# Block inverses on GpSimd instead of VectorE, the cubic on VectorE, and first blocks turned by VectorE transposes

## The chip, the core and the metric

One core of a Trainium2 chip runs the whole program. Five engines work side by side, each with its own in-order queue: TensorE (PE, with its weight loads PEld), VectorE (DVE), ScalarE (ACT), GpSimd (POOL) and SyncE (SP), which issues most DMAs. The metric is device time in microseconds of one launch, the median of several runs.

## The reference

Three layers follow each other, in float32. The first is delta-rule attention over 768 positions, for 4 batches of 8 heads with dimension 48; per position t

```python
v_old = np.einsum('bhde,bhd->bhe', state, kt)
state = state + bt[:, :, :, None] * np.einsum('bhd,bhe->bhde', kt, vt - v_old)
```

with normalised keys and output `q . state` taken ahead of the update. Its output, 3072 tokens of 384 values, goes through an expert layer of width 2048 with a rational activation, g = (a0 + a1 h + a2 h^2 + a3 h^3) / (1 + |b0| |h| + |b1| h^2 + 1e-6), and then through a second one with g = max(h, 0)^2.

## The kernel before

**Attention.** The sequence is cut into 12 chunks of 64 positions. A chunk of one batch is a step n (48 steps, all 8 heads together), and 8 steps are a group g (6 groups, `attention(g)`). In a chunk the recurrence becomes a solve with a triangular 64 x 64 matrix; per group its 32 x 32 diagonal blocks are inverted, one block in each partition of Tt, by elimination. For groups 2 to 5 that is 31 steps of two operations on DVE (L471 the product into tmp, L472 the subtraction from Tt), with a x b columns, a = s + 1, b = 31 - s; each needs the one before. For groups 0 and 1 the inversion stops at 16 x 16 blocks (15 steps, L462 and L464), and matmuls merge them (`ma`, `mb`, `mc`, L528 to L552, in halves hf). The inverses lie one per partition and are needed as matmul operands, so Tt goes to DRAM (td) and comes back with rows on partitions (L490, L505 into TT); its transpose, which ACT makes in Gb (L491), goes by nd to DN or TN (L508 to L516). Matmuls L578 and L591 with copies L584 and L596 give the 32 x 32 block below the diagonal. Then the steps run: `first`, `middle` (copies L699, masks on POOL L703), `rest` (L724, L738, L743), which write the tokens into xin. The Gram matrices of later groups (L425 and `gram`) go by Gs and DRAM to Gb.

**Layers 1 and 2.** Tokens are taken 512 at a time (i, 6 blocks), hidden units 128 at a time (j, 16). A unit (i, j) of layer 1 is 9 matmuls into a PSUM bank of pool h (3 banks; L866), the rational activation, and 3 second matmuls of full float32 (L904) into three accumulators. In `rational`, ACT makes |h| (L883), a copy hs of h in SBUF (L884) and b0 + b1|h| (L885); POOL multiplies that by |h| (L886), and makes a2 + a3 h (L887) and its product with h (L889) from hs; DVE adds a1 and multiplies (L890), ACT makes 1/Q by Ln and Exp (L891, L892), DVE does the last three operations (L893 to L895). Layer 2 starts when layer 1 is done; its weights are split by ACT and POOL (L824 to L832) ahead of it.

**Order.** All work is entered as tasks by `add(engine, cost, function, r, w, due, ...)`. `Plan.run` plays the list with the costs given, per engine, by due times; it repeats that 8 times, each time with due times worked back from the last play, and emits the instructions in the order of the best one. So each engine's order is fixed when the program is built. A task with `lock=1` on DVE and one on POOL never overlap in the plan. `inv_due(g)` asks for group g's inverse some 90 to 10 us ahead of unit block g - 1, `step_due` spreads the steps over block g - 1. In planned PE gaps of the prologue `PL.fill` puts matmuls on a constant tile (L284, filler).

Of the kernel before, what the change touches and what calls it, by code (L numbers as in the profile page):

```python
# [19 lines left out]
C = 64  # L20
# [15 lines left out]
ROUNDS = 8  # L36
# [11 lines left out]
class Plan:  # L48
# [38 lines left out]
    def run(self):  # L87
# [22 lines left out]
        lo, hi, one, dur = self.fill  # L110
# [116 lines left out]
def kernel(ctx, tc, kT, kS, qT, kn, vn, beta, par_in, w1, w2, outT):  # L227
# [56 lines left out]
    PL.fill = (T0 - 55, T0 + 20, lambda: nc.tensor.matmul(banks[2][:, 0:N // 2], ones[:, 0:128], ones, start=True, stop=True), 0.11)  # L284
# [11 lines left out]
    tiny = at.tile([128, 1], F32, name="tiny")  # L296
    be = at.tile([128, 32], F32, name="be")
# [6 lines left out]
    tiles(at, "kTc", 3, [128, NP, C])  # L304
# [33 lines left out]
    add("POOL", 1.0, eye, w=["ident"], due=15)  # L338
    add("POOL", 1.0, lambda: P_.memset(Nb, 0.0), w=[("N", o) for o in range(0, 128, 32)], due=3)
# [38 lines left out]
    for n in range(8):  # L378
# [22 lines left out]
        add("ACT", 0.6, o2, r=[key], w=[("TN", 32), ("TN", 96)], due=n + 8, free=[key])  # L401
# [12 lines left out]
    def gstore(n, due):  # L414
        add("ACT", 0.37, lambda: A_.copy(slot["Gs", n], ps(("G", n), [128, NP, C])), r=[("G", n)], w=[("Gs", n)], due=due,
            alloc=(("Gs",), ("Gs", n)), free=[("G", n)])
        dma(128, gs[n // 8][:, n % 8], lambda: slot["Gs", n], r=[("Gs", n)], w=[("gs", n)], due=due, free=[("Gs", n)])

    def attention(g):
# [70 lines left out]
        dma(512, td[g], Tt, r=["Tt"], w=[("td", g)], due=d1, lat=2.0)  # L490
        add("ACT", 2.05, lambda: A_.copy(Gb, Tt.rearrange("p a b -> p b a")), r=["Tt"], w=GB, due=d1)  # L491
# [10 lines left out]
        for i in (1, 0):  # L502
# [17 lines left out]
        for hf in range(2 if g < 2 else 0):  # L520
            ka, kb, kc = ("mA", g, hf), ("mB", g, hf), ("mC", g, hf)

            def ma(hf=hf):
                w = ps(("mA", g, hf), [128, 4, NP, 32])
                for s in range(4):
                    for p in range(NP):
                        for o in range(0, 128, 32):
                            M.matmul(w[o:o + 32, s, p], Nb[o:o + 32, 4 * hf + s, p], TTg[o:o + 32, 4 * hf + s, p, o % 64:o % 64 + 32],  # L528
                                     start=True, stop=True)
# [36 lines left out]
            add("PE", 1.3, mc, r=["E"] + dn_, w=[kc], due=dd, alloc=(pl, kc), free=["merge"])
            add("ACT", 1.2, mco, r=[kc], w=[("TNh", hf, 0), ("TNh", hf, 1)], due=dd, free=[kc])


        for hf in range(2):  # L570
# [29 lines left out]
            add("PE", 1.3, m1, r=g21 + [("TTx", g % 2, 1, 0), ("TTx", g % 2, 1, 1), ("TD", g % 2, hf)], w=[kw], due=dd, alloc=(pl, kw))  # L600
            add("ACT", 1.2, m1o, r=[kw], w=["ws"], due=dd, free=[kw])
            add("PE", 1.3, m2, r=[("TN", 0), ("TN", 64), ("TNh", hf, 0), ("TNh", hf, 1), "ws"], w=[kt_], due=dd, alloc=(pl, kt_))
            add("ACT", 1.2, m2o, r=[kt_], w=[("T", g % 2, hf)], due=dd, free=[kt_],
                after=[i for x in range(2) for i in [PL.last["TTx", g % 2, 0, x]]])

# [68 lines left out]
        def first(k, k2, due):  # L674
# [201 lines left out]
    def rational(i, j, due):  # L876
# [3 lines left out]
        hk, ak, bk, ck, gk, sk = (x + (u,) for x in (("h",), ("a",), ("b",), ("c",), ("g",), ("hs",)))  # L880
        h, a, b, c, g, hs = (lambda k=k: slot[k] for k in (hk, ak, bk, ck, gk, sk))
# [3 lines left out]
        add("ACT", 0.83, lambda: A_.activation(b(), a(), AF.Identity, bias=s(4), scale=s(5)), r=[ak, "par"], w=[bk], due=due + 3.8, alloc=(("b",), bk))  # L885
        add("POOL", 1.32, lambda: P_.tensor_tensor(b(), b(), a(), op=ALU.mult), r=[ak], w=[bk], due=due + 5, lock=1)  # L886
# [164 lines left out]
```

## Time and profile before

| | us |
|---|---|
| median of 3 runs (1182.72 to 1186.74) | 1183.78 |
| the profiled execution | 1189.82 |
| its span | 1188.1 |
| PE busy in it | 1088.5 (92%) |
| DVE busy | 716.0 (60%) |
| ACT busy | 676.3 (57%) |
| POOL busy | 459.2 (39%) |
| mean granted PE clock | 0.945 |

The profiled execution is one of its own, so sums made from its rows stand against 1189.82. A span includes all from the first to the last instruction. Line numbers (L471) are those of the kernel before. In the chain of waits, a piece "DMA" is a transfer that something waited for, "SPq" time in SP's queue, "issue" time in which an engine waited for nothing that the profile shows.

### The profile page before, as it was taken

How to read it: one execution, taken by the hardware profiler on the slowest of the kernel's cores; microseconds unless marked ns; L12 is line 12 of the kernel's file. 1: busy time of each engine (PE TensorE's matmuls, PEld its weight loads, DVE VectorE, ACT ScalarE, POOL GpSimd, SP SyncE). 2: the span in 40 equal slices, each digit the busy share in tenths (PEclk: the TensorE clock that was granted, in tenths of full speed). 3: DMA queues.
4: the chain of work that ended last, by engine and by line, in shares of the span. 5: the costliest groups of instructions: out<-in, count | busy, mean ns of one | idle time of the engine just before them, and what ended most of it. 6: DMA issues, size and time to landing. Idle time of an engine off the chain costs nothing.

```text
span 1188.1 us, 24846 instructions
## 1 busy us (share of the span) xinstructions
PE 1088.5 (92%) x10030; PEld 769.2 (65%) x10030; DVE 716.0 (60%) x1237; ACT 676.3 (57%) x1269; POOL 459.2 (39%) x479
## 2 busy tenths in 40 slices
PE   4687898799897998998899989999999999999998
PEld 4576565456554555655566646567788888888887
DVE  4353777887888689668755546788633343333432
ACT  5365876586667576765576867766523333243432
POOL 3304654476564565565456648735300000000000
PEclk7668998799998899998999999999999999999999
DMA  7756324461226033502130022144100001000000
GB/s 223 175 186 162 85 65 144 142 152 40 84 80 126 15 86 87 109 9 59 54 81 17 20 83 80 33 154 138 67 9 27 27 18 36 1 27 1 27 1 27
DMA packets 135394, 87.83 MB, mean 74 GB/s; under 512 B 102384, under 2 KB 119920, under 8 KB 135280
## 3 DMA queue, kind: packets, MB, share of 16 engines
q1 hardware_dynamic: 134992, 85.20, 26.0%
q8 instruction: 79, 1.29, 0.5%
q10 hardware_dynamic: 288, 1.05, 0.2%
q14 instruction: 35, 0.29, 0.1%
HBM read 64.98 MB, written 19.92 MB: 71 GB/s over the span
## 4 chain that ended last, share of the span: by engine, by line
PE 72%; DVE 8%; issue 5%; DMA 4%; ACT 4%; POOL 3%; SPq 3%; ACTq 0%; POOLq 0%; DVEq 0%
PE bank L866 28%; PE bank L904 18%; PE bank L930 5%; PE bank L928 5%; PE bank L929 5%; PE bank L666 5%; SPq L316 3%; DVE tmp L471 2%; PE bank L724 2%; DVE Tt L472 2%; POOL A L825 1%; POOL C L832 1%; DMA kTg<-in_kS_dram 1%; DVE mem L893 1%; PE bank L578 1%
## 5 line engine op out<-in xcount | busy, mean ns | idle before, releaser
L866 PE MATMUL bank<-xh,A 128*128 128x512 f32 x1152 | 362.8, 396 | 3.6 <-POOL A L825 3.6
L904 PE MATMUL bank<-mem,B 128*128 128x512 f32 x576 | 289.0, 635 | 22.1 <-DVE mem L895 21.1
L866 PE MATMUL bank<-xl,A 128*128 128x512 f32 x576 | 258.7, 449 | 11.0 <-DVE mem L895 6.5
L866 PEld LDWEIGHTS bank<-xh,A 128*128 128x128 f32 x1152 | 219.9, 191 | 67.0 <-issue 15.1
L904 PEld LDWEIGHTS bank<-mem,B 128*128 128x128 f32 x576 | 107.6, 198 | 126.3 <-issue 88.7
L916 DVE SCALAR_TENSOR_TENSOR mem<-bank,mem 128x512 f32<-128x512 f32 x96 | 66.3, 691 | 152.2 <-ACT mem L915 152.1
L887 POOL TENSOR_SCALAR mem<-hs,par 128x512 f32<-128x512 f32 x96 | 79.6, 829 | 176.8 <-ACT hs L884 140.5
L866 PEld LDWEIGHTS bank<-xl,A 128*128 128x128 f32 x576 | 110.1, 191 | 54.3 <-issue 14.8
L915 ACT ACTIVATE mem<-bank 128x512 f32<-128x512 f32 x96 | 57.5, 599 | 152.2 <-PE bank L866 152.1
L886 POOL TENSOR_TENSOR mem<-mem 128x512 f32<-128x512 f32 x96 | 126.4, 1317 | 9.3 <-DVE mem L893 4.2
L889 POOL TENSOR_TENSOR mem<-mem,hs 128x512 f32<-128x512 f32 x96 | 125.4, 1306 | 7.4
L930 PE MATMUL bank<-gh,C 128*128 128x512 f32 x288 | 113.7, 395 | 0.0
L928 PE MATMUL bank<-gl,C 128*128 128x512 f32 x288 | 113.5, 394 | 0.0
L929 PE MATMUL bank<-gh,C 128*128 128x512 f32 x288 | 112.0, 389 | 0.0
L893 DVE SCALAR_TENSOR_TENSOR mem<-mem,par,bank 128x512 f32<-128x512 f32 x96 | 71.5, 745 | 61.0 <-ACT bank L892 60.6
L890 DVE SCALAR_TENSOR_TENSOR mem<-mem,par,bank 128x512 f32<-128x512 f32 x96 | 71.1, 741 | 59.4 <-POOL mem L889 56.0
L919 DVE TENSOR_TENSOR gl<-mem,gh 128x512 fp32r<-128x512 f32 x96 | 69.2, 722 | 60.0 <-ACT gh L918 60.0
L918 ACT CAST gh<-mem 128x512 fp32r<-128x512 f32 x96 | 59.6, 621 | 70.9 <-DVE mem L916 59.8
L883 ACT ACTIVATE mem<-bank 128x512 f32<-128x512 f32 x96 | 57.4, 598 | 73.2 <-PE bank L866 72.1
L891 ACT ACTIVATE mem<-mem,par 128x512 f32<-128x512 f32 x96 | 69.2, 721 | 29.2 <-POOL mem L886 28.5
L885 ACT ACTIVATE mem<-mem,par 128x512 f32<-128x512 f32 x96 | 78.5, 817 | 0.9
L703 POOL TENSOR_SCALAR_AFFINE_SELECT X<-X 64x256 f32<-64x256 f32 x96 | 42.0, 438 | 71.1 <-ACT X L699 64.4
(119 smaller groups left out, 1636.7 us busy)
## 6 DMA issues: line engine op xcount, KB each, us to landing
raw<-in_w_dram SPq DMA_DIRECT2D x18, 768.0 KB, 5.3
B<-in_w_dram SPq DMA_DIRECT2D x10, 768.0 KB, 4.8
kTg<-in_kS_dram SPq DMA_DIRECT2D x40, 128.0 KB, 2.9
gs<-Gs SPq DMA_DIRECT2D x40, 128.0 KB, 2.6
kTc<-in_kT_dram SPq DMA_DIRECT2D x40, 128.0 KB, 2.1
kn<-in_kn_dram SPq DMA_DIRECT2D x12, 384.0 KB, 3.7
X<-in_qT_dram SPq DMA_DIRECT2D x96, 48.0 KB, 2.4
vn<-in_vn_dram SPq DMA_DIRECT2D x12, 384.0 KB, 3.2
```

The lines of the kernel that those rows point to most:

```text
L866: M.matmul(h, a, b, start=(k == 0 and m == 0), stop=(k == NK - 1 and m == 2))
L885: add("ACT", 0.83, lambda: A_.activation(b(), a(), AF.Identity, bias=s(4), scale=s(5)), r=[ak, "par"], w=[bk], due=due + 3.8, alloc=(("b", ...
L886: add("POOL", 1.32, lambda: P_.tensor_tensor(b(), b(), a(), op=ALU.mult), r=[ak], w=[bk], due=due + 5, lock=1)
L887: add("POOL", 0.85, lambda: P_.tensor_scalar(c(), hs(), s(3), s(2), op0=ALU.mult, op1=ALU.add), r=[sk, "par"], w=[ck], due=due + 5, lock=1 ...
L889: add("POOL", 1.32, lambda: P_.tensor_tensor(c(), c(), hs(), op=ALU.mult), r=[sk], w=[ck], due=due + 6.5, lock=1, free=[sk])
L890: add("DVE", 0.775, lambda: V.scalar_tensor_tensor(c(), c(), s(1), h(), op0=ALU.add, op1=ALU.mult), r=[hk, "par"], w=[ck], due=due + 7.3)
L891: add("ACT", 0.72, lambda: A_.activation(a(), b(), AF.Ln, bias=s(6)), r=[bk, "par6"], w=[ak], due=due + 7)
L893: add("DVE", 0.775, lambda: V.scalar_tensor_tensor(c(), c(), s(0), h(), op0=ALU.add, op1=ALU.mult), r=[hk, "par"], w=[ck], due=due + 9)
L904: M.matmul(acc[d], Bw[j][:, 128 * d:128 * d + 128], slot[gk], start=(j == 0), stop=(j == NJ - 1))
L928: M.matmul(acc[d], wh, gl, start=(j == 0), stop=False)
L929: M.matmul(acc[d], wl, gh, start=False, stop=False)
L930: M.matmul(acc[d], wh, gh, start=False, stop=(j == NJ - 1))
```

## The change

- The 62 elimination operations of groups 2 to 5 are issued on GpSimd, as two tasks a step.
- In `rational` the copy hs goes. ACT makes a2 + a3 h from the PSUM bank into c, DVE multiplies c by h from the bank; the rest is as before. Due times of the later operations come up to 1 us earlier.
- Groups 0 and 1: td, nd and their ten DMAs go. Two DVE transposes turn the 16 x 16 inverses: from Tt to Gb (then the moving operand of `ma`) and to DN. For group 0 the block Nb is made by ACT, Dg times a column `half` of zeros and ones, in place of four DMAs.
- For group 0 the copies from PSUM with o >= 64 go to DVE (`move`), as does L398; for the others they stay on ACT. Each partition range is a task of its own.
- The transposed keys kTc get a fourth buffer (hs's space is free). Filler matmuls: other constants; `FILL` is 0, so the added minimum does nothing.

```diff
-ROUNDS = 8
+ROUNDS, FILL = 8, 0
...
                 gap = T[i]["s"] - max(end, lo)
-                if gap > 0.6 and T[i]["s"] < hi:
-                    for _ in range(int(0.7 * (gap - 0.2) / dur)):
-                        one()
+                n = int((gap - 0.2) / dur) if gap > 0.5 and T[i]["s"] < hi else 0
+                for _ in range(max(n, least if lo + 6 < T[i]["s"] < T0 - 4 else 0)):
+                    one()
...
-    tiles(one, "hs", 2, [128, N])
...
-    PL.fill = (T0 - 55, T0 + 20, lambda: ..., 0.11)
+    PL.fill = (T0 - 64, T0 + 20, lambda: ..., 0.16, FILL)
...
-    tiles(at, "kTc", 3, [128, NP, C])
+    tiles(at, "kTc", 4, [128, NP, C])
...
+    def halves():
+        P_.memset(half, 1.0)
+        for o in range(0, 128, 32):
+            P_.affine_select(half[o:o + 32], half[o:o + 32], pattern=[[0, 1]], base=-16, channel_multiplier=1, compare_op=ALU.is_ge, fill=0.0)
+    add("POOL", 0.6, halves, w=["half"], due=5)
...
-                A_.copy(TN[o:o + 32, n], t[o:o + 32, :, 0:32])
+                V.tensor_copy(TN[o:o + 32, n], t[o:o + 32, :, 0:32])
...
+    def move(g, o, dur, get, f=None, **kw):
+        def act():
+            a, b = get()
+            A_.copy(a, b) if f is None else A_.mul(a, b, f)
+        def dve():
+            a, b = get()
+            V.tensor_copy(a, b) if f is None else V.tensor_scalar(a, b, f, None, op0=ALU.mult)
+        add(*(("DVE", dur, dve) if g == 0 and o >= 64 else ("ACT", dur, act)), **kw)
...
         for s in range(31 if g > 1 else 0):
             a, b = s + 1, 31 - s
-            def st(s=s, a=a, b=b):
+            def st1(s=s, a=a, b=b):
                 tv = tmp[:, :a * b].rearrange("p (a b) -> p a b", a=a)
-                V.tensor_tensor(tv, _mid(Gb[:, s, s + 1:32], [128, a, b]), Tt[:, 0:a, s:s + 1].to_broadcast([128, a, b]), op=ALU.mult)
-                V.tensor_tensor(Tt[:, 0:a, s + 1:32], Tt[:, 0:a, s + 1:32], tv, op=ALU.subtract)
-            add("DVE", 0.42 + 2.0e-3 * a * b, st, r=GB, w=["Tt", "tmp"], due=d1, lock=1)
+                P_.tensor_tensor(tv, _mid(Gb[:, s, s + 1:32], [128, a, b]), Tt[:, 0:a, s:s + 1].to_broadcast([128, a, b]), op=ALU.mult)
+            def st2(s=s, a=a, b=b):
+                tv = tmp[:, :a * b].rearrange("p (a b) -> p a b", a=a)
+                P_.tensor_tensor(Tt[:, 0:a, s + 1:32], Tt[:, 0:a, s + 1:32], tv, op=ALU.subtract)
+            for st in (st1, st2):
+                add("POOL", 0.17 + 2.3e-3 * a * b, st, r=GB, w=["Tt", "tmp"], due=d1, lock=1)
...
-        if g < 2:
+        if g == 0:
+            add("ACT", 0.85, lambda: A_.mul(Nb.rearrange("r s p c -> r (s p) c")[:, :, 0:16], Dg.rearrange("r s p c -> r (s p) c")[:, :, 0:16], half),
+                r=[("Dg", n) for n in range(8)] + ["half"], w=[("N", o) for o in range(0, 128, 32)], due=d1)
+        elif g == 1:
...
-        dma(512, td[g], Tt, r=["Tt"], w=[("td", g)], due=d1, lat=2.0)
-        add("ACT", 2.05, lambda: A_.copy(Gb, Tt.rearrange("p a b -> p b a")), r=["Tt"], w=GB, due=d1)
+        if g < 2:
+            add("DVE", 2.0, lambda: V.transpose(Gb.rearrange("r q c -> r c q"), Tt.rearrange("p a b -> p b a")), r=["Tt"], w=GB, due=d1, lock=1)
+            add("DVE", 2.0, lambda: V.transpose(DN.rearrange("r s p c -> r c (s p)"), Tt), r=["Tt"], w=["DN"], due=d1 + 1, lock=1)
+        else:
+            dma(512, td[g], Tt, r=["Tt"], w=[("td", g)], due=d1, lat=2.0)
+            add("ACT", 2.05, lambda: A_.copy(Gb, Tt.rearrange("p a b -> p b a")), r=["Tt"], w=GB, due=d1)
...
-        for i in (1, 0):
+        for i in (1, 0) if g > 1 else ():
...
-        if g < 2:
-            sk = add("ACT", 0.4, lambda: A_.dma_start(nd[g], Gb), r=GB, due=d1)
-            ...
-        else:
+        if g > 1:
...
-                            M.matmul(w[o:o + 32, s, p], Nb[o:o + 32, 4 * hf + s, p], TTg[o:o + 32, 4 * hf + s, p, o % 64:o % 64 + 32],
-                                     start=True, stop=True)
+                            M.matmul(w[o:o + 32, s, p], Nb[o:o + 32, 4 * hf + s, p], Gb[o:o + 32, 16 * hf + 4 * s + p], start=True, stop=True)
...
-            add("ACT", 2.4, mbo, r=[kb] + tx, w=[("TD", g, hf)], due=dd, free=[kb])
+            for o in (32, 96, 0, 64):
+                move(g, o, 0.6, lambda o=o, f=mbo: f(o), r=[kb], w=[("TD", g, hf, o)], due=dd, free=[kb], after=[PL.last[wT[0]]])
...
-        add("ACT", 0.62, lambda: A_.copy(hs(), h()), r=[hk], w=[sk], due=due + 3, alloc=(("hs",), sk))
+        add("ACT", 0.79, lambda: A_.activation(c(), h(), AF.Identity, bias=s(2), scale=s(3)), r=[hk, "par"], w=[ck], due=due + 4.5, alloc=(("c",), ck))
         add("POOL", 1.32, lambda: P_.tensor_tensor(b(), b(), a(), op=ALU.mult), ...)
-        add("POOL", 0.85, lambda: P_.tensor_scalar(c(), hs(), s(3), s(2), op0=ALU.mult, op1=ALU.add), ...)
-        add("POOL", 1.32, lambda: P_.tensor_tensor(c(), c(), hs(), op=ALU.mult), ...)
+        add("DVE", 0.69, lambda: V.tensor_tensor(c(), h(), c(), op=ALU.mult), r=[hk], w=[ck], due=due + 5.5)
```

The other lines of the diff carry the new task names through the reads, writes and waits of `m1`, `m2` and `first`, and shift due times in `rational`.

## Rows read from the trace of the kernel before

**Rows 1.** Stages: length; PE, PEld, DVE, ACT, POOL busy (x); clock; DMA share; GB/s.
```profile
0.00:113.00 113.00, 76.30 (x1999) 65.92 (x1999) 51.37 (x136) 58.14 (x134) 32.35 (x60) 0.70 0.69 184
113.00:262.00 149.00, 127.92 (x2057) 83.40 (x2057) 111.50 (x208) 103.74 (x196) 81.05 (x80) 0.91 0.47 126
262.00:612.00 350.00, 320.28 (x3293) 195.75 (x3291) 271.24 (x493) 234.41 (x457) 196.78 (x203) 0.96 0.28 69
612.00:700.00 88.00, 87.52 (x716) 53.39 (x715) 50.35 (x86) 63.00 (x124) 53.49 (x58) 1.00 0.10 29
700.00:790.00 90.00, 83.45 (x266) 50.45 (x265) 60.39 (x83) 64.93 (x106) 61.80 (x54) 0.98 0.26 85
790.00:1189.00 399.00, 392.99 (x1709) 320.32 (x1707) 171.14 (x233) 152.06 (x255) 33.78 (x27) 1.00 0.10 35
```

**Rows 2.** Chain of waits, 80 to 125: start us, length us, what.
```profile
...
86.03 3.20 DMA nd<-Gb
...
113.03 4.30 PE bank L866 x18
...
```

**Rows 3.** Chain of waits, 262 to 612: share of it by line.
```profile
by line: PE bank L904 28.7%; PE bank L866 19.2%; PE bank L666 7.3%; DVE tmp L471 5.6%; SPq L316 5.2%; DVE Tt L472 4.6%; issue 3.3%; PE bank L724 2.8%; DMA Gb<-gs 2.6%; DVE mem L895 2.1%; DVE mem L893 2.0%; DVE bank L894 1.8%; ACT Gb L491 1.
```

**Rows 4.** Waits over the span: total us, times, longest us.
```profile
...
PE bank L904 <- DVE mem L895: 21.1, 13, 4.5
...
```

**Rows 5.** Single lines: count, shortest/median/longest ns, first and last start.
```profile
L471 DVE TENSOR_TENSOR tmp<-Gb,Tt x124: 179/404/1508, 145.6 to 593.1; 128x31 f32<-128x31 f32 x8, 128x60 f32<-128x60 f32 x8, 128x87 f32<-128x87 f32 x8, 128x112 f32<-128x112 f32 x8
L893 DVE SCALAR_TENSOR_TENSOR mem<-mem,par,bank x96: 731/747/749, 123.1 to 780.5; 128x512 f32<-128x512 f32 x96
L886 POOL TENSOR_TENSOR mem<-mem x96: 1262/1287/2012, 120.4 to 777.8; 128x512 f32<-128x512 f32 x96
L825 POOL TENSOR_TENSOR A<-raw,A x10: 1012/1019/1350, 107.1 to 244.8; 128x384 fp32r<-128x384 f32 x10
```

**Rows 6.** DVE in order of time: start us, length us, operation.
```profile
...
310.98 1.38 DVE L471 TENSOR_TENSOR tmp<-Gb,Tt 128x247 f32<-128x247 f32 x1
312.39 1.36 DVE L472 TENSOR_TENSOR Tt<-Tt,tmp 128x247 f32<-128x247 f32 x1
...
330.17 0.40 DVE L471 TENSOR_TENSOR tmp<-Gb,Tt 128x247 f32<-128x247 f32 x1
...
```

**Rows 7.** Groups of instructions: busy us, mean ns | idle before them.
```profile
...
L889 POOL TENSOR_TENSOR mem<-mem,hs 128x512 f32<-128x512 f32 x96 | 125.4, 1306 | 7.4
...
L887 POOL TENSOR_SCALAR mem<-hs,par 128x512 f32<-128x512 f32 x96 | 79.6, 829 | 176.8 <-ACT hs L884 140.5 <-issue 34.5 <-POOL X L703 0.9
...
L885 ACT ACTIVATE mem<-mem,par 128x512 f32<-128x512 f32 x96 | 78.5, 817 | 0.9
...
L472 DVE TENSOR_TENSOR Tt<-Tt,tmp 128x31 f32<-128x31 f32 (+15 forms) x124 | 63.0, 508 | 4.3
...
L471 DVE TENSOR_TENSOR tmp<-Gb,Tt 128x31 f32<-128x31 f32 (+15 forms) x124 | 62.8, 506 | 1.9
...
L884 ACT COPY hs<-bank 128x512 f32<-128x512 f32 x96 | 56.0, 584 | 12.2 <-PE bank L866 11.8
...
L491 ACT COPY Gb<-Tt 128x1024 f32<-128x1024 f32 x6 | 12.1, 2018 | 8.1 <-DVE Tt L472 8.1
...
L545 ACT COPY TT<-bank 32x512 f32<-32x512 f32 x16 | 9.2, 576 | 7.9 <-PE bank L540 7.7
...
```

**Rows 8.** POOL in order of time, 117 to 121.
```profile
118.32 0.77 POOL L887 TENSOR_SCALAR mem<-hs,par 128x512 f32<-128x512 f32 x1 [7.55 <-ACT hs L884]
119.18 1.29 POOL L889 TENSOR_TENSOR mem<-mem,hs 128x512 f32<-128x512 f32 x1
...
```

**Rows 9.** DVE and PE in order of time, prologue.
```profile
...
15.23 1.94 DVE L435 STREAM_TRANSPOSE Gb<-TT 128x1024 f32<-128x1024 f32 x1
...
29.75 0.21 DVE L464 TENSOR_TENSOR Tt<-Tt,tmp 128x30 f32<-128x30 f32 x1
...
43.27 2.64 PE L528 MATMUL bank<-TT,mem 32*32 32x32 f32 x239
...
```

More of the change, by code (lines that the diff above doesn't have):

```diff
@@ L109, in run @@
             t["s"], t["e"] = s, e
-        lo, hi, one, dur = self.fill
+        lo, hi, one, dur, least = self.fill
         end = 0.0
@@ L296 @@
     tiny = at.tile([128, 1], F32, name="tiny")
+    half = at.tile([128, 1], F32, name="half")
     be = at.tile([128, 32], F32, name="be")
@@ L599, in attention @@
             g21 = [("TN", 32), ("TN", 96)]
[L600 to L604, printed above, removed]
+            td_ = [("TD", g, hf, o) for o in range(0, 128, 32)] if g < 2 else []
+            add("PE", 1.3, m1, r=g21 + [("TTx", g % 2, 1, 0), ("TTx", g % 2, 1, 1)] + td_, w=[kw], due=dd, alloc=(pl, kw))
+            for o in (0, 64):
+                move(g, o, 0.6, lambda o=o, f=m1o: f(o), -1.0, r=[kw], w=[("ws", o)], due=dd, free=[kw])
+            add("PE", 1.3, m2, r=[("TN", 0), ("TN", 64), ("TNh", hf, 0), ("TNh", hf, 1), ("ws", 0), ("ws", 64)], w=[kt_], due=dd, alloc=(pl, kt_))
+            for o in (0, 64):
+                move(g, o, 0.6, lambda o=o, f=m2o: f(o), r=[kt_], w=[("T", g % 2, hf, o)], due=dd, free=[kt_],
+                     after=[PL.last["TTx", g % 2, 0, x] for x in range(2)] if g > 1 else [PL.last[wT[0]]])
         pl = ("att",) if g else ("att", "h")
@@ L885, in rational @@
-        add("ACT", 0.83, lambda: A_.activation(b(), a(), AF.Identity, bias=s(4), scale=s(5)), r=[ak, "par"], w=[bk], due=due + 3.8, alloc=(("b",), bk))
-        add("POOL", 1.32, lambda: P_.tensor_tensor(b(), b(), a(), op=ALU.mult), r=[ak], w=[bk], due=due + 5, lock=1)
-        add("POOL", 0.85, lambda: P_.tensor_scalar(c(), hs(), s(3), s(2), op0=ALU.mult, op1=ALU.add), r=[sk, "par"], w=[ck], due=due + 5, lock=1,
-            alloc=(("c",), ck))
-        add("POOL", 1.32, lambda: P_.tensor_tensor(c(), c(), hs(), op=ALU.mult), r=[sk], w=[ck], due=due + 6.5, lock=1, free=[sk])
@@ L890, in rational @@
-        add("DVE", 0.775, lambda: V.scalar_tensor_tensor(c(), c(), s(1), h(), op0=ALU.add, op1=ALU.mult), r=[hk, "par"], w=[ck], due=due + 7.3)
-        add("ACT", 0.72, lambda: A_.activation(a(), b(), AF.Ln, bias=s(6)), r=[bk, "par6"], w=[ak], due=due + 7)
-        add("ACT", 0.62, lambda: A_.activation(h(), a(), AF.Exp, scale=-1.0), r=[ak], w=[hk], due=due + 8, free=[ak])
-        add("DVE", 0.775, lambda: V.scalar_tensor_tensor(c(), c(), s(0), h(), op0=ALU.add, op1=ALU.mult), r=[hk, "par"], w=[ck], due=due + 9)
@@ L894, in rational @@
-        add("DVE", 0.72, lambda: V.scalar_tensor_tensor(h(), b(), 1.0 + EPS, h(), op0=ALU.add, op1=ALU.mult), r=[bk], w=[hk], due=due + 9.8, free=[bk])
-        add("DVE", 0.72, lambda: V.scalar_tensor_tensor(g(), h(), -2.0, c(), op0=ALU.add, op1=ALU.mult), r=[hk, ck], w=[gk], due=due + 10.6,
+        add("ACT", 0.83, lambda: A_.activation(b(), a(), AF.Identity, bias=s(4), scale=s(5)), r=[ak, "par"], w=[bk], due=due + 3.3, alloc=(("b",), bk))
+        add("ACT", 0.79, lambda: A_.activation(c(), h(), AF.Identity, bias=s(2), scale=s(3)), r=[hk, "par"], w=[ck], due=due + 4.5, alloc=(("c",), ck))
@@ new lines, in rational @@
+        add("POOL", 1.32, lambda: P_.tensor_tensor(b(), b(), a(), op=ALU.mult), r=[ak], w=[bk], due=due + 4.2, lock=1)
+        add("DVE", 0.69, lambda: V.tensor_tensor(c(), h(), c(), op=ALU.mult), r=[hk], w=[ck], due=due + 5.5)
+        add("DVE", 0.75, lambda: V.scalar_tensor_tensor(c(), c(), s(1), h(), op0=ALU.add, op1=ALU.mult), r=[hk, "par"], w=[ck], due=due + 6.3)
+        add("ACT", 0.72, lambda: A_.activation(a(), b(), AF.Ln, bias=s(6)), r=[bk, "par6"], w=[ak], due=due + 6)
+        add("ACT", 0.62, lambda: A_.activation(h(), a(), AF.Exp, scale=-1.0), r=[ak], w=[hk], due=due + 7, free=[ak])
```

55 lines of the change are left out of this document (25 added, 30 removed).

## The prediction

> **What bounds the kernel now.** I cut the span into stages first [rows 1]. The prologue lasts to 113 us, when the first layer-1 matmul runs [rows 2]; layer 1 goes on to about 790, layer 2 to the end. TensorE (PE) stands idle 36.7 us in the prologue, 21.1 in 113 to 262, 29.7 in 262 to 612, 0.5 in 612 to 700, 6.5 in 700 to 790 and 5.1 in the 398 us after that (length less PE busy). Layer 2 is PE work at clock 1.00; the change can take little there. The granted clock is 0.91 in 113 to 262 and 0.96 in 262 to 612: of its two levels (1.2 and 2.4 GHz) the lower one holds part of the time, and counted as (1 - clock) x length that is 13.4 and 14.0 us. So layer 1 has 21.1 + 13.4 + 29.7 + 14.0 + 6.5 = 85 us that are not PE at full speed (idle and clock overlap in part, so this is an upper end).
>
> The stretch 612 to 700 is a control. It holds layer-1 units and recurrence steps of the last attention group, but no 32-step inverse, for the last one ends before it. There PE is idle 0.5 of 88 us at clock 1.00, with DVE busy 57%. In 262 to 612, with three inverses, DVE is busy 271.2 of 350 (77%). The chain of that stretch [rows 3] has 10.2% of its length, 36 us, on the inverse's two DVE lines L471 and L472, and the longest wait of the second matmuls is for DVE's last rational operation, 21.1 us in 13 waits of the whole span [rows 4]. So in the inverse windows VectorE's in-order queue sets the pace: the inverse fills the queue in which the activation that feeds L904 stands.
>
> Why is it so long? The 124 executions of L471 take 179 to 1508 ns [rows 5]. With 247 columns one takes 1.38 us while POOL works on tensors, with the same columns 0.40 later [rows 6]. A DVE operation with one operand in PSUM shows none of this: L893 lies between 731 and 749 ns in all 96 [rows 5]. By the two ends (179 ns at 31 columns, 0.40 us at 247) DVE alone costs about 147 ns + 1.02 ns a column; an inverse has 62 operations over 2 x 5,456 = 10,912 columns, 20 us. It takes (62.8 + 63.0)/4 = 31.4 [rows 7]. So 11 us of each inverse are waits for POOL.
>
> The Trainium skill (SBUF — State Buffer, "SBUF: two separate sides") says the pair of ports that VectorE and GpSimd share is an exclusive lock, taken by a VectorE operation with two SBUF inputs against a GpSimd one that reads SBUF. The rows of L471 and L893 fit it. It also speaks against the change: with the inverse on POOL the lock is held more often, and DVE's weight conversions in the first pass have two SBUF inputs. By it the worst case is full alternation.
>
> **The change, part by part.** *The inverse on GpSimd (groups 2 to 5).* No row shows an operation of this shape on POOL. The nearest are its subtraction and product: 1012 ns at 384 columns, 1262 at 512 [rows 5], which gives 1.95 ns a column and 262 ns fixed. An inverse: 62 x 0.262 + 10,912 x 0.00195 = 16.2 + 21.3 = 37.5 us; a POOL operation that needs the one before starts 0.09 us after its end (118.32 + 0.77 = 119.09, the next at 119.18 [rows 8]), 62 x 0.09 = 5.6. I take 43 us; bounds 20 (DVE's price) and 94 (62 x 1.508, the upper end of L471). POOL loses L887 and L889, 0.829 + 1.306 = 2.14 us a unit [rows 7], 102 us over the 48 units of 262 to 612, and gains 3 x 37.5 = 112: 196.8 becomes about 207 busy of 350. No saturation; but 62 dependent operations a block stand among L886 and the masks L703, each of which can wait one operation, 0.26 to 0.76 us.
>
> The Trainium skill (GPSIMD Engine Reference, "When to use GPSIMD") puts two-input elementwise work on VectorE, GpSimd being about 2x slower. Alone the rows agree (43 against 20 us), against the contended 31.4 it is 1.4x. By that rule alone the chain of an inverse grows by 12 us; the sum here rests on where it stands, which is off DVE's queue.
>
> *The cubic on DVE.* A unit loses ACT's copy L884 (0.584) and gains an ACT activation priced like L885 (0.817): +0.23 us. DVE gains one product of PSUM and SBUF; nearest L893 at 0.747, I take 0.70. DVE in 262 to 612: 271.2 - 94 + 48 x 0.70 = 211 of 350 (60%, near the control's 57%). ACT: 234.4 + 11 = 246 of 350, 77% if the stretch shrinks to 320. The unit's path also gets shorter: the constant, quadratic and cubic terms leave POOL, so L886 is no longer queued with 2.14 us of others, and a PSUM bank comes free sooner (the 6.5 us of 700 to 790).
>
> *What that gives.* 262 to 612: idle and clock 43.7. The control says nearly all of it can go; but ACT is busier, and the inverse still hangs on its loads. I take two thirds, -28; bounds 0 and -44. 113 to 262: 34.5, with one inverse, but also the conversions of the weights, and the gaps of the first merge, which stay; I take two fifths, -14; bounds 0 and -30. 612 to 790: -3; bounds 0 and -7. Layer 2: 0 (bounds +2 and -4: freed POOL splits its weights earlier).
>
> *The first two groups' blocks.* Now the last small step ends at 29.96 and the first merge matmul starts at 43.27 [rows 9]; between them lie ACT's turn L491 (2.02 us [rows 7]), DMAs to DRAM and four back. After: one DVE transpose, 1.94 us as L435 [rows 9], and the merge can start near 32; the second is hidden behind the first matmuls. That is 11 us. For group 1 the DMA of L491's result lay on the chain (86.03, 3.20 us [rows 2]) with L491 ahead of it, 5 us more; that turn goes to DVE too. Splitting PSUM copies of 0.576 us [rows 7] between ACT and DVE gives some 2. Against it: PE's queue is in order, and gram matmuls that wait for loads stand in it; queries' loads and the weights may be late next. I take -10; bounds 0 and -18. *Edits at nothing:* the fourth buffer for transposed keys, the filler's constants (about as many fillers per us of planned gap: 0.7/0.11 against 1/0.16), the half mask on an idle POOL, and the copies L398 on an idle DVE; if not hidden, under 2 us together.
>
> **Sum.** Against the profiled execution (1189.8 = span 1188.1 and 1.7 around it): -10 - 14 - 28 - 3 = -55, 1135. The median shown, 1183.8, is 6.0 below that execution, so 1129. The bounds add up to +2 and -103; I don't expect all at one end.
>
> **The rivals.** *Another bound takes the place of DVE.* For it: the chain of 262 to 612 also goes through SP's queue and the loads of Gb (5.2% and 2.6% [rows 3]), which stay, and ACT rises to 77%. Then the stalls of layer 1 shrink by a fifth only: -10 - 7 - 9 = -26, 1158. Against it: the control stretch has ACT at 72% and no stall. *Nothing in net:* the prologue's gain is eaten by in-order waits, and the longer inverse delays the recurrence as much as DVE gains: 1184. *Slower: POOL becomes the bound.* Place: blocks 1 to 4 of layer 1. POOL's other work is (196.8 - 102)/3 = 31 us a block, a block lasts 117 now; POOL decides once an inverse costs over 117 - 31 = 86 us, twice my price, as it would with operations stretched to 1.4 us as DVE's were [rows 6]. At 94 each block would be 125, four of them +32, less 10: 1206. Against it: POOL's own products lie mostly near their shortest (1287 median, 1262 shortest [rows 5]), so POOL is rarely the one held.
>
> The Trainium skill's lock names this case: in the first pass DVE's conversions and POOL's inverse would take turns. Even one after the other they are within the 149 us of that stretch, so the time from the rows stands.
>
> **How the numbers follow.** Forecast 0.66 (its own range 1100 to 1148), another bound 0.20, nothing in net 0.06, slower 0.08. The range leaves out the slower case and the far end: 1098 to 1168. A difference of 0.3%, 3.6 us, is about what can be told from no change. Faster 0.87, same 0.05, slower 0.08.
>
> **What would show it.** Right: PE idle in 262 to 612 falls below 12 us and the clock there rises to 0.98; L471's successors on POOL average 0.6 us and make 43 us an inverse when not interrupted; the wait of L904 for DVE falls under 8 us; the first layer-1 matmul comes near 103. Wrong: POOL operations of the inverse over 0.9 us on average; masks L703 or L886 waiting in POOL's queue with PE idle behind them; a start of layer 1 still at 113, with loads ending the waits; or ACT as the new last releaser.

## The result, and the profile after

The changed kernel takes 1125.57 us (median of 4 runs, 1123.39 to 1128.77), the kernel before 1184.92 on the same chip (4 runs, 1182.72 to 1186.74): ratio 0.9502, 95% interval 0.9469 to 0.9535. The profiled execution took 1127.35 us with a span of 1125.6. In the text a line is that of the kernel it is told of; in the changed kernel L887 is the first layer-1 matmul (L866 before), L923 the second (L904), L488 and L492 the two operations of the inverse (L471, L472), L907 POOL's product (L886), L906 and L908 the cubic's new operations on ACT and DVE.

First the page of the changed kernel, part 1 (busy time, share of the span, instructions) and the shares of the chain that ended last:

```profile
PE 1065.3 (95%) x10076; PEld 761.6 (68%) x10076; DVE 673.7 (60%) x1115; ACT 684.3 (61%) x1242; POOL 387.8 (34%) x540
...
PE 84%; ACT 4%; DVE 3%; issue 2%; POOL 0%; DMA 0%; SPq 0%; DVEq 0%; ACTq 0%; POOLq 0%
```

A tuned kernel is best compared by stages. A block here is the 16 units of layer 1 for 512 tokens. I cut both spans where DVE ends the last of the three operations on xl that prepare a block's tokens, since the block's matmuls start about then; the last block ends with DVE's last rational operation. The windows of the changed kernel follow: prologue, block 0, blocks 1 to 3, block 4, block 5, layer 2. Columns are stretch and length; busy us (instructions) of PE, PEld, DVE, ACT and POOL; granted PE clock; DMA share; GB/s.

```profile
0.00:94.00 94.00, 66.40 (x2125) 59.10 (x2125) 59.04 (x147) 42.28 (x101) 27.76 (x58) 0.75 0.62 180
94.00:239.00 145.00, 123.93 (x1888) 82.90 (x1889) 104.50 (x170) 101.08 (x188) 87.86 (x113) 0.92 0.42 119
239.00:540.00 301.00, 298.70 (x3265) 187.07 (x3263) 208.41 (x356) 244.03 (x451) 186.67 (x288) 1.00 0.34 83
540.00:639.00 99.00, 98.47 (x822) 60.34 (x823) 67.52 (x113) 78.21 (x143) 28.13 (x33) 1.00 0.08 22
639.00:721.00 82.00, 76.74 (x241) 46.18 (x241) 63.70 (x95) 64.32 (x102) 29.01 (x24) 0.98 0.26 90
721.00:1126.00 405.00, 401.03 (x1739) 326.06 (x1737) 170.58 (x238) 154.39 (x259) 28.39 (x24) 1.00 0.10 37
```

And the same first stages of the kernel before, cut in the same way (its stages in [rows 1] were cut at other moments):

```profile
0.00:111.00 111.00, 74.30 (x1965) 64.39 (x1966) 49.37 (x133) 57.77 (x133) 32.35 (x60) 0.70 0.67 184
111.00:254.00 143.00, 122.16 (x1947) 79.74 (x1946) 106.68 (x197) 97.44 (x185) 74.88 (x75) 0.90 0.48 126
254.00:598.00 344.00, 314.61 (x3155) 192.15 (x3154) 271.11 (x497) 229.35 (x450) 194.65 (x200) 0.96 0.28 70
```

| stage | before, us | after, us | difference |
|---|---|---|---|
| prologue | 111.3 | 94.3 | -17.0 |
| block 0 | 142.8 | 145.3 | +2.5 |
| block 1 | 113.0 | 100.9 | -12.1 |
| block 2 | 115.5 | 100.4 | -15.1 |
| block 3 | 115.5 | 99.3 | -16.2 |
| block 4 | 98.9 | 98.5 | -0.4 |
| block 5 | 85.7 | 82.3 | -3.4 |
| layer 2 | 405.4 | 404.7 | -0.7 |
| span | 1188.1 | 1125.6 | -62.5 |

Read it so: in blocks 1 to 3 PE stood idle 29.4 us before (344.0 less 314.6) at clock 0.96; after it is idle 2.3 at 1.00. Of the 43 us, 27 are idle time and 16 are less busy time (314.6 against 298.7 us), PE's work being done at the higher clock. All three blocks now come within 2.4 us of block 4, the control without an inverse. The groups of the changed kernel show the mechanism (busy us, mean ns of one, then idle time ahead and what ended it):

```profile
L923 PE MATMUL bank<-mem,B 128*128 128x512 f32 x576 | 278.6, 613 | 4.1 <-DVE mem L914 1.7 <-ACT mem L904 1.5 <-DVE B L836 0.9
L907 POOL TENSOR_TENSOR mem<-mem 128x512 f32<-128x512 f32 x96 | 123.3, 1286 | 203.6 <-ACT mem L905 203.0
L906 ACT ACTIVATE mem<-bank,par 128x512 f32<-128x512 f32 x96 | 73.6, 769 | 0.7
L492 POOL TENSOR_TENSOR Tt<-Tt,tmp 128x31 f32<-128x31 f32 (+15 forms) x124 | 70.3, 567 | 8.5
L488 POOL TENSOR_TENSOR tmp<-Gb,Tt 128x31 f32<-128x31 f32 (+15 forms) x124 | 66.1, 533 | 20.1 <-DVE Tt L473 12.1
L908 DVE TENSOR_TENSOR mem<-bank,mem 128x512 f32<-128x512 f32 x96 | 65.8, 686 | 57.5 <-ACT mem L906 57.2
```

The second matmuls' wait for DVE fell from 21.1 us [rows 4] to 1.7. An inverse costs POOL (66.1 + 70.3)/4 = 34.1 us. The new line L908 by itself (shortest/median/longest ns, first and last start):

```profile
L908 DVE TENSOR_TENSOR mem<-bank,mem x96: 647/690/694, 115.1 to 716.5; 128x512 f32<-128x512 f32 x96
```

With one operand in PSUM it never lengthens, though POOL now runs the inverse beside it; compare L893 and L471 in [rows 5].

The first layer-1 matmul, in PE's timeline of the changed kernel (start, us, instruction), comes at 95.95 instead of 113.0. But 30 us later, in block 0, PE waits for the second group's merge, and the first layer-1 matmul behind that comes at 134.76:

```profile
95.95 0.50 PE L887 MATMUL bank<-xl,A 128*128 128x512 f32 x1
...
127.06 1.93 PE L560 MATMUL bank<-mem,DN 32*32 32x32 f32 x128 [4.43 <-DVE mem L553]
...
134.76 0.80 PE L887 MATMUL bank<-xl,A 128*128 128x512 f32 x1
```

### The profile page after: what moved, and what is told of

The parts are those of the page before. It is cut to its first block, busy times and chain, and to the rows that moved or that the text cites. A ratio compares the mean times of both kernels' runs of the same rounds, so it can differ in the third digit from the quotient of the medians.

```text
span 1125.6 us, 24712 instructions
## 1 busy us (share of the span) xinstructions
PE 1065.3 (95%) x10076; PEld 761.6 (68%) x10076; DVE 673.7 (60%) x1115; ACT 684.3 (61%) x1242; POOL 387.8 (34%) x540
## 4 chain that ended last, share of the span: by engine, by line
PE 84%; ACT 4%; DVE 3%; issue 2%; POOL 0%; DMA 0%; SPq 0%; DVEq 0%; ACTq 0%; POOLq 0%
PE bank L887 34%; PE bank L923 21%; PE bank L949 6%; PE bank L947 6%; PE bank L948 6%; PE bank L686 5%; PE bank L745 2%; PE bank L597 1%; PE bank L609 1%; ACT mem L905 1%; ACT xin L759 1%; ACT mem L906 0%; DVE X L764 0%; ACT X L720 0%; DVE bank L913 0%
## 5 line engine op out<-in xcount | busy, mean ns | idle before, releaser
L887 PE MATMUL bank<-xh,A 128*128 128x512 f32 x1152 | 360.6, 394 | 1.1 <-POOL A L846 1.1
L923 PE MATMUL bank<-mem,B 128*128 128x512 f32 x576 | 278.6, 613 | 4.1 <-DVE mem L914 1.7
L887 PE MATMUL bank<-xl,A 128*128 128x512 f32 x576 | 257.6, 447 | 5.3 <-DVE mem L914 5.3
L887 PEld LDWEIGHTS bank<-xh,A 128*128 128x128 f32 x1152 | 218.4, 190 | 63.4 <-issue 16.0
L907 POOL TENSOR_TENSOR mem<-mem 128x512 f32<-128x512 f32 x96 | 123.3, 1286 | 203.6 <-ACT mem L905 203.0
L923 PEld LDWEIGHTS bank<-mem,B 128*128 128x128 f32 x576 | 103.8, 192 | 96.9 <-issue 78.7
L887 PEld LDWEIGHTS bank<-xl,A 128*128 128x128 f32 x576 | 109.1, 189 | 47.2 <-issue 15.3
L912 DVE SCALAR_TENSOR_TENSOR mem<-mem,par,bank 128x512 f32<-128x512 f32 x96 | 71.4, 743 | 67.0 <-ACT bank L911 66.8
L908 DVE TENSOR_TENSOR mem<-bank,mem 128x512 f32<-128x512 f32 x96 | 65.8, 686 | 57.5 <-ACT mem L906 57.2
L904 ACT ACTIVATE mem<-bank 128x512 f32<-128x512 f32 x96 | 57.0, 595 | 47.5 <-PE bank L887 46.6
L906 ACT ACTIVATE mem<-bank,par 128x512 f32<-128x512 f32 x96 | 73.6, 769 | 0.7
L492 POOL TENSOR_TENSOR Tt<-Tt,tmp 128x31 f32<-128x31 f32 (+15 forms) x124 | 70.3, 567 | 8.5
L488 POOL TENSOR_TENSOR tmp<-Gb,Tt 128x31 f32<-128x31 f32 (+15 forms) x124 | 66.1, 533 | 20.1 <-DVE Tt L473 12.1
```

Of the source, the lines that this page charges most:

```text
L492: P_.tensor_tensor(Tt[:, 0:a, s + 1:32], Tt[:, 0:a, s + 1:32], tv, op=ALU.subtract)
L887: M.matmul(h, a, b, start=(k == 0 and m == 0), stop=(k == NK - 1 and m == 2))
L906: add("ACT", 0.79, lambda: A_.activation(c(), h(), AF.Identity, bias=s(2), scale=s(3)), r=[hk, "par"], w=[ck], due=due + 4.5, alloc=(("c", ...
L912: add("DVE", 0.75, lambda: V.scalar_tensor_tensor(c(), c(), s(0), h(), op0=ALU.add, op1=ALU.mult), r=[hk, "par"], w=[ck], due=due + 8)
L923: M.matmul(acc[d], Bw[j][:, 128 * d:128 * d + 128], slot[gk], start=(j == 0), stop=(j == NJ - 1))
```

## The experiments

**One part at a time.** Theory: VectorE's queue was the bound of blocks 1 to 3, and the inverse's move takes it away; rival: either move does most of it alone. The first kernel puts the inverse back on DVE and keeps the rest of the change.

```diff
-                P_.tensor_tensor(tv, ...); ...
-                add("POOL", 0.17 + 2.3e-3 * a * b, st, ..., lock=1)
+                V.tensor_tensor(tv, ...); V.tensor_tensor(Tt..., op=ALU.subtract)
+            add("DVE", 0.42 + 2.0e-3 * a * b, st, ..., lock=1)
```

> The changed kernel (1125.6) with the inverses of groups 2 to 5 back on VectorE; cubic and prologue as changed. Theory (the inverse fills VectorE's in-order queue): VectorE then has both, 271 + 48 x 0.69 = 304 us of the 350 us of unit blocks 1 to 3, so those blocks stay at 113 us or grow; with the prologue's 17 us the time is 1160 to 1185. L471's mean falls from 507 ns to about 420, since POOL has 2.14 us less a unit with which to hold it up. Rival (the gain comes from the unit's shorter path, the cubic off POOL): unit blocks 1 to 3 come to 103 us or less, time under 1140.

Measured 1169.76 us, 0.9853 (0.9818 to 0.9888): the theory's time, not the rival's. Its groups and its blocks 1 to 3:

```profile
L919 PE MATMUL bank<-mem,B 128*128 128x512 f32 x576 | 286.4, 630 | 9.8 <-DVE mem L910 7.9 <-DVE B L832 1.1 <-DVE nT L471 0.8
...
L489 DVE TENSOR_TENSOR Tt<-Tt,tmp 128x31 f32<-128x31 f32 (+15 forms) x124 | 48.6, 392 | 4.2
L488 DVE TENSOR_TENSOR tmp<-Gb,Tt 128x31 f32<-128x31 f32 (+15 forms) x124 | 42.7, 345 | 1.6
```

```profile
251.50:582.00 330.50, 307.16 (x3204) 191.32 (x3203) 264.34 (x535) 238.37 (x446) 93.27 (x103) 0.96 0.32 74
```

With half of POOL's work in these blocks gone (93.3 us, before 194.7) the same operations on DVE take 368 ns on average ((42.7 + 48.6)/248; expected 420), before 507 ((62.8 + 63.0)/248 [rows 7]): the part that was waiting for POOL shrinks when POOL does less. An inverse is 22.8 us, near the prediction's 20 for DVE alone. But DVE has the cubic now as well and stays at 264.3 of 330.5 us, 80%, and PE waits.

The second kernel keeps the inverse on POOL and puts the cubic back there.

```diff
-        add("ACT", 0.79, lambda: A_.activation(c(), h(), ...)); add("DVE", 0.69, ... c(), h(), c() ...)
+        add("ACT", 0.62, lambda: A_.copy(hs(), h()), ...)
+        add("POOL", 0.85, lambda: P_.tensor_scalar(c(), hs(), s(3), s(2), ...), ..., lock=1)
+        add("POOL", 1.32, lambda: P_.tensor_tensor(c(), c(), hs(), op=ALU.mult), ..., lock=1)
```

> The changed kernel with the cubic back on POOL (a copy of h by ACT, two POOL operations) and the inverses on POOL; kTc has 3 buffers again for space. Theory: VectorE is free (211 - 34 = 178 of 350 us), but POOL holds 197 + 102 = 299 of 350: unit blocks 1 to 3 at 103 to 112 us, POOL the releaser of the waits, time 1135 to 1155. Rival (shorter path): blocks stay at 113, time 1165 or more.

Measured 1197.12 us, 1.0082 (1.0057 to 1.0107): 0.8% slower than before. The theory's 1135 to 1155 is missed, and the rival's 113 us a block doesn't come either (329/3 = 110). Block 0 and blocks 1 to 3 of it, and the wait of DVE's next operation for POOL's cubic product (us in all, times, longest; the second line is the same wait in the kernel before):

```profile
92.00:272.00 180.00, 142.17 (x1954) 91.75 (x1953) 105.23 (x162) 100.90 (x194) 123.90 (x146) 0.83 0.36 100
272.00:601.00 329.00, 301.77 (x3255) 189.40 (x3255) 174.32 (x304) 228.97 (x448) 279.90 (x383) 0.98 0.32 75
```

```profile
DVE mem L912 <- POOL mem L911: 88.9, 47, 10.6
DVE mem L890 <- POOL mem L889: 56.0, 30, 10.5
```

POOL is busy 85% of blocks 1 to 3, and each unit's cubic stands in its queue among the inverse. Even so these blocks are 15 us shorter than before (344.0); the loss lies in block 0, which lasts 179.7 us (before 142.8).

The third has neither move, only the new prologue. Theory: the earlier start carries through; rival: it is given back in block 0.

```diff
-                P_.tensor_tensor(tv, ...); ...
+                V.tensor_tensor(tv, ...); ...
...
-        add("DVE", 0.69, ... c(), h(), c() ...)
+        add("POOL", 1.32, ... c(), c(), hs() ...)
```

> Only the prologue's part of the change: transposes and split copies of the first two groups, filler constants; inverse on VectorE and cubic on POOL as before. Theory (parts add up): first layer-1 matmul near 96 us as in the changed kernel, unit blocks 1 to 3 near 115 us, time 1185 - 17 = 1168. Rival (the earlier start is given back in the first pass, which waits for weights and group 1's merge): first matmul at 96 but unit block 0 longer, time 1178 to 1185.

Measured 1187.88 us, 1.0012 (0.9992 to 1.0031): no difference, the rival. The start is as early as in the changed kernel (first line below, PE's timeline), but block 0 lasts 160.8 us and ends at 258.7, later than before (254.1). Its windows for block 0 and blocks 1 to 3 follow; PE is busy 12 us longer in block 0 than before, at clock 0.84 instead of 0.90, and idle 6 us longer.

```profile
96.72 0.50 PE L884 MATMUL bank<-xl,A 128*128 128x512 f32 x1 [1.76 <-DVE xl L868]
```

```profile
97.00:258.00 161.00, 134.62 (x1926) 87.66 (x1927) 123.12 (x217) 98.00 (x188) 84.60 (x81) 0.84 0.43 113
258.00:596.00 338.00, 310.46 (x3129) 191.04 (x3122) 263.09 (x496) 230.68 (x451) 197.17 (x200) 0.98 0.28 69
```

So, with the new prologue in all four, in medians and with the length and busy shares of blocks 1 to 3 and the length of block 0:

| inverse on | cubic on | us | blocks 1 to 3, us | DVE | POOL | block 0, us |
|---|---|---|---|---|---|---|
| DVE | POOL | 1187.9 | 337.4 | 78% | 58% | 160.8 |
| DVE | DVE | 1169.8 | 330.5 | 80% | 28% | 158.5 |
| POOL | POOL | 1197.1 | 328.7 | 53% | 85% | 179.7 |
| POOL | DVE | 1125.6 | 300.6 | 69% | 62% | 145.3 |

The cubic's move alone is worth -18.1, the inverse's alone +9.2, both -62.3. The remaining -53 is their interaction (-48 in the profiled executions): the change is an exchange of work. In blocks 1 to 3 each move alone gives 7 to 9 us and both give 37, so 21 of the interaction lie there, and only the exchange leaves both queues short of 70%. The larger part, 32 us, lies in block 0, where DVE also converts the layer-1 weights and POOL splits them. PE waits there for a weight tile (A) 6.9, 10.7 and 12.1 us in the first three kernels and 1.1 in the changed one; why the conversions come in time only there was not tried. Nor was a kernel that takes work off DVE and puts none on POOL.

**The prologue the other way round.** The kernel before, with only the inverse and the cubic changed (and kTc's fourth buffer); the old prologue stays.

```diff
-            add("DVE", 0.42 + 2.0e-3 * a * b, st, ..., lock=1)
+            for st in (st1, st2):
+                add("POOL", 0.17 + 2.3e-3 * a * b, st, ..., lock=1)
...
+        add("ACT", 0.79, ... c() from h() ...); add("DVE", 0.69, ... c(), h(), c() ...)
```

> Inverse on POOL, cubic on VectorE and four kTc buffers as changed; the first two groups' blocks, copies and filler constants as before the change. Theory A (the prologue's 17 us are given back in unit block 0, as they were when the prologue changed alone): time 1122 to 1130, the same as the whole change; first matmul at 113, block 0 at 128 us or so. Theory B (with the other two parts done the earlier start is worth what it shows): first matmul at 113, block 0 at 145, time 1140 to 1143.

Measured 1127.31 us, 0.9492 (0.9458 to 0.9526), the same as the whole change, as theory A has it. Its first layer-1 matmul comes 10 us later than the changed kernel's 95.95, and its block 0 ends at 238.6 against 239.6. (It was expected at 113: the old prologue in a new order starts 7 us earlier than before.)

```profile
106.15 0.80 PE L869 MATMUL bank<-xl,A 128*128 128x512 f32 x1
```

**What holds block 0's end.** First theory: ACT makes group 1's copies from PSUM in the middle of the first units (DVE idles 9.7 us ahead of L908 at 115 us, waiting for ACT), so give half of them to DVE, as group 0 has it.

```diff
-        add(*(("DVE", dur, dve) if g == 0 and o >= 64 else ("ACT", dur, act)), **kw)
+        add(*(("DVE", dur, dve) if g < 2 and o >= 64 else ("ACT", dur, act)), **kw)
```

> The changed kernel, with half of the copies of group 1's merge on VectorE too, as group 0's are. In the changed kernel unit block 0 takes 145 us and three units stand ready from 106 to 130 us while ACT makes group 1's copies, VectorE idle for 9.7 us of it. Theory (ACT's copies of the merge hold up the first units' activation): block 0 falls by 4 to 8 us, time 1118 to 1122. Rival (block 0 hangs on the weights): no change, 1125.

Measured 1130.64 us, 0.9528 (0.9491 to 0.9566), block 0 150.4: no gain, the theory falls. Second theory: DVE's conversion of the layer-1 weights, most of it in block 0 (14 of the 16 steps L834, all 16 of L836). This kernel leaves two of its steps out for layer 1 (the sign operation and the shift for the first matrix), so its values differ.

```diff
+            if l == 2:
                 add("DVE", 1.0, lambda: V.scalar_tensor_tensor(lo(), hi(), 0x80000000, ...), ..., lock=1)
...
-            add("DVE", 0.6, lambda: V.scalar_tensor_tensor(lo()[:, si], hi()[:, si], 3, ...), ..., lock=1)
```

> The changed kernel; of the conversion of layer 1's weights two VectorE operations a block are left out (the sign, and the shift for the first matrix), so the weights' values are wrong: 1.5 us less VectorE work for each of 16 blocks. Theory (unit block 0 hangs on the conversion of weights in VectorE's queue): block 0 falls from 145 to 125 to 132 us, time 1105 to 1113. Rival (it hangs on group 1's merge and recurrence steps): block 0 over 140 us, time 1120 to 1126.

Measured 1118.25 us, 0.9419 (0.9373 to 0.9466). Block 0 of it, which has 104.5 us of DVE work in the changed kernel:

```profile
100.40:223.40 123.00, 115.03 (x1719) 73.52 (x1717) 80.86 (x141) 99.77 (x185) 80.48 (x112) 0.93 0.46 132
```

Block 0 falls from 145.3 to 123.0 and ends 16 us earlier, so the conversion is in its path. The median falls by 7 only, less than expected. The profiled execution is the slowest of the four (1124.8; the fastest took 1112.1), and in it block 1 is 5.5 us and block 3 3.5 us longer than in the changed kernel.

**How much POOL can take.** The prediction had POOL decide from 86 us an inverse. The product L488 is issued twice, the same result written again.

```diff
-            for st in (st1, st2):
+            for st in (st1, st1, st2):
```

> The changed kernel with each product of the inverse of groups 2 to 5 made twice on POOL (the same values): 62 operations become 93, an inverse 34.1 + 16.5 = 51 us, POOL busy in unit blocks 1 to 3 about 187 + 50 = 237 of 301 us (79%). Theory (POOL decides only once it is nearly full; the cubic on POOL was slow because it stood in the unit's own path): under 1% slower, blocks 1 to 3 at 100 to 102, time 1125 to 1134. Rival (POOL's occupancy alone made the cubic on POOL slow, at 280 of 329, 85%): blocks 1 to 3 at 104 to 108, time 1140 or more.

Measured 1161.64 us, 0.9786 (0.9757 to 0.9815), 36 us above the changed kernel: the theory falls, and the time is the rival's (1140 or more). Its blocks 1 to 3 and the inverse's lines:

```profile
258.00:574.00 316.00, 308.04 (x3278) 192.00 (x3278) 208.43 (x352) 241.95 (x452) 233.97 (x384) 0.97 0.33 76
```

```profile
L488 POOL TENSOR_TENSOR tmp<-Gb,Tt 128x31 f32<-128x31 f32 (+15 forms) x248 | 129.5, 522 | 31.1 <-DVE Tt L473 14.9
...
L492 POOL TENSOR_TENSOR Tt<-Tt,tmp 128x31 f32<-128x31 f32 (+15 forms) x124 | 69.4, 560 | 8.7
```

An inverse is now (129.5 + 69.4)/4 = 49.7 us of POOL work, far below 86, and POOL is busy 74%; yet from its first operation to its last the one in block 0 takes 99 us and the others 81 to 83 (in the changed kernel 91 and 55 to 56). The loss shows in block 0, which starts 9 us and ends 18.6 us later, and in blocks 1 and 2, 14.3 us longer together. In blocks 1 to 3 PE is idle 8.0 us (2.3 in the changed kernel) and busy 8.8 us longer, at clock 0.97; 5.1 us of the idle time are waits for the inverse's way back through DRAM (TN from nd), and only 0.2 are waits for POOL.

Why already at 74%? One theory: Gb and Tt are single, so group g + 1's inverse can't begin until g's has been read. The odd groups from 3 on get buffers of their own, first with the product twice, then without.

```diff
+    Gb2 = at.tile([128, 32, 32], F32, name="Gb2")
+        p2 = g % 2 if g > 1 else 0
+        Gb, Tt, tk = (GbA, TtA, "Tt") if p2 == 0 else (Gb2, DN.rearrange("r s p c -> r (s p) c"), "DN")
```

> The kernel with each product of the inverse made twice (1161.6 us), and groups 3 and 5 with a Gb and a Tt of their own (Tt in DN, which only groups 0 and 1 use; kTc has 3 buffers for space). Theory (the loop: an inverse lasts 85 to 95 us from first to last operation, then Tt must be stored and Gb loaded again, some 20 us, before the next begins, so a unit block can't be shorter than 105 to 110): with two buffers blocks 1 and 2 fall from 107 and 109 to 100 to 103, time 1145 to 1152 (block 0 and the start as they are). Rival (POOL's occupancy: L907 and the masks stand behind the inverse's operations): blocks 1 and 2 stay at 105 or more, time 1158 or more.

> The changed kernel with two buffers for Gb and Tt in the same way (kTc 3). Its inverses last 58 us and 42 us lie between two of them. Theory (loop): nothing to gain in blocks 1 to 3, 99 to 101 each, time 1120 to 1130. Rival (the reload of Gb still holds up the blocks): under 1115.

Measured 1162.31 us, 0.9797 (0.9741 to 0.9852), and 1127.19 us, 0.9507 (0.9461 to 0.9552): nothing in either. In the first the inverses still take 79 to 82 us (the one in block 0 110) with 20 to 42 us between them, so the buffers were not what kept them apart.

**Is it only another order?** The plan is made anew for each kernel, so a lucky order is a rival to all of the above. One kernel is the kernel before whose plan is told what the inverse really costs on DVE; the other the changed kernel with 32 rounds of planning in place of 8.

```diff
-            add("DVE", 0.42 + 2.0e-3 * a * b, st, ...)
+            add("DVE", 0.55 + 3.0e-3 * a * b, st, ...)
...
-ROUNDS, FILL = 8, 0
+ROUNDS, FILL = 32, 0
```

> The kernel before, but the plan is told 0.55 + 0.003 a b for a step of the inverse on VectorE (1.08 us on average, what the trace of before shows with its gaps) in place of 0.42 + 0.002 a b (0.77). Only the order changes. Theory (the engine is short of time, not the order wrong): within 1% of before, 1175 to 1195. Rival (the plan was misled and the change's gain is a better order): half of the gain or more, under 1155.

> The changed kernel, the list of tasks played 32 times in place of 8 for its order; the same instructions. Both theories: within 1%, 1115 to 1137; it shows how much an order alone moves. A rival to all (the gain of the change is a lucky order): over 1140.

Measured 1201.46 us, 1.0121 (1.0077 to 1.0165), and 1129.13 us, 0.9509 (0.9451 to 0.9567). Order alone moved the old kernel by 1.2%, for the worse and a little more than expected, and the new one by nothing that can be told. Every kernel here has an order of its own: the five with both moves and the whole computation, each product made once, lie at 1126 to 1131 us, the three with neither at 1185 to 1201. A lucky order doesn't make that gap.

None of these kernels beats the changed one with the whole computation in it.

## Why the prediction was right, and where it was not

*What bounds the kernel: right, as far as it goes.* In blocks 1 to 3 the waits of the second matmuls for DVE went and the blocks fell to the control's length, as forecast. But DVE relieved by the inverse's move alone (53% busy) still left 328.7 us there, with POOL at 85% and its lines over a quarter of that stretch's chain of waits: DVE's queue was the bound, and POOL's takes its place unless the cubic leaves it. The inverse's waits for POOL are shown by the first experiment (507 to 368 ns). The Trainium skill ("SBUF — State Buffer", section "SBUF: two separate sides") describes the lock of the shared ports between VectorE and GpSimd; the runs agree, by these two means and by L908, which reads one operand from PSUM and stays within 647 to 694 ns.

*Blocks 1 to 3, -28: right in kind, too small.* They gave 43.4 us, nearly all that was taken for the upper bound (43.7 of idle and clock in 262 to 612). The control, block 4 at 98.9, was the better forecast: the blocks came to 100.9, 100.4 and 99.3. The third held back for ACT and for the loads of Gb was not needed. ACT rose to 244.0 of 301 us (81%; forecast 77) and the second matmuls waited 1.5 us for it in the whole span. The signs named for being right came: PE idle 2.3 us at clock 1.00, POOL's operations 0.55 us on average, the wait for DVE 1.7 us, and the start at 95.95, earlier than the 103 named.

*The price of the inverse: slightly high.* Forecast 37.5 us of operations, measured 34.1. The line drawn from 384 and 512 columns doesn't hold at small sizes. POOL's timeline in the first pass of the changed kernel shows two at 192 columns, 0.52 and 0.58 us, where the line gives 0.64, with 0.08 us between them:

```profile
130.01 0.52 POOL L488 TENSOR_TENSOR tmp<-Gb,Tt 128x192 f32<-128x192 f32 x1
130.61 0.58 POOL L492 TENSOR_TENSOR Tt<-Tt,tmp 128x192 f32<-128x192 f32 x1
```

The cubic's operations were forecast 0.70 (DVE) and 0.817 (ACT) and took 0.686 and 0.769.

*The prologue, -10: this step failed.* The first layer-1 matmul came 17 us earlier, more than forecast, and that was worth nothing: block 0 took it back. The sum added the start's gain to the first pass as if the two were independent, but the start is not what holds block 0's end. In three kernels with both moves (second buffers, changed kernel, old prologue) block 0 starts at 92.5, 94.3 and 104.1 us and ends at 238.9, 239.6 and 238.6; with 32 rounds and with group 1's copies on DVE it starts at 95.5 and 95.4 and ends at 241.9 and 245.8. DVE's conversions of the weights are part of what holds it, and the earlier start leaves more of them behind it: DVE has the first matrix of 6 of the 16 weight blocks ready when block 0 starts in the kernel before and in the one that keeps its prologue, of 2 in the four of the table.

*The first pass, -14: right in size, seen from the end of block 0.* The stage table shows +2.5 only because the earlier start is booked above it. Between the prologue-only kernel and the changed one block 0 falls from 160.8 to 145.3, by 15.5; in the kernel with the old prologue it ends 15.5 us earlier than before as well. Prologue and first pass together gave 14.5, not 24. The 15 more in blocks 1 to 3 and the 10 missing here partly cancel, so that the total is close (forecast -55, measured -62.5 in the profiled span) is in part luck. *The rest, -3:* measured -4.5.

*The rival of POOL as the bound: unlikely for the right reason, but with a wrong threshold.* It was put at 86 us an inverse, the point at which POOL has no free time left. At 49.7 us the kernel had lost 36 us. So POOL's queue cost time well before it was full. A likely way is that a chain of dependent operations stands in one queue with L907 and the masks, each of which it holds up and is held up by. That this is how 74% busy becomes 81 to 99 us an inverse is argued, not shown; only the single buffers were tried, and they were not it. The prediction also didn't see that the inverse's move alone is slower than before.

## What to carry to other kernels

Price the move of work between two in-order queues by both queues' load afterwards: here each half of an exchange was worth -18 and +9 us, both -62. In blocks 1 to 3 only the exchange left both below 70%; look at every stage, for the larger part of what the halves lacked lay in block 0. A stretch of the same kernel without the suspect, such as block 4 here, is the best forecast of what is left when it is gone; take it whole unless a row says otherwise. An earlier start is worth nothing where the next stage has an end of its own, so look for what sets that end first.

## What the runs showed of the hardware that was not expected

Small two-operand operations on POOL are cheaper than the line through its large ones: 237 ns for the shortest of L488 (31 columns; the line gives 322), median 550, as the rows of one line show:

```profile
L488 POOL TENSOR_TENSOR tmp<-Gb,Tt x124: 237/550/1407, 122.6 to 507.2; 128x31 f32<-128x31 f32 x8, 128x60 f32<-128x60 f32 x8, 128x87 f32<-128x87 f32 x8, 128x112 f32<-128x112 f32 x8
```

The longest, 1407 ns, shows that POOL is stretched too, but on average less than DVE was. The shortest execution of each size, added up over an inverse's 62 operations, makes 31.8 us on POOL and 20.8 on DVE; the average one took 34.1 on POOL, and on DVE 31.4 before and 22.8 with half of POOL's work gone. The Trainium skill (GPSIMD Engine Reference, "When to use GPSIMD") puts such work on VectorE; as a single move the run agrees (1.0082), in exchange for an operation with an operand in PSUM it does not (0.9502).
